# Retention in chunks of 64 tokens: four products on quarters of the PE array, a compact state summed by DVE

## The chip, the cores and the metric

One Trainium2 chip, one of its cores. A time is the device time of one execution in microseconds (us); smaller is better. The kernel before takes 1517.68 us, the median of three runs (1516.84 to 1517.86). TensorE is called PE in the profile, VectorE DVE, ScalarE ACT, GpSimd POOL, and SyncE, which issues the DMAs, SP.

## What is computed

Eight batches of eight heads, 576 tokens, head size 64. Retention is attention without softmax, with a decay that depends on the head; two mixing layers follow.

```python
scores = scale * np.matmul(q, k.transpose(0, 1, 3, 2))
Dmat = np.where(rel >= 0, gamma[:, None, None] ** rel[None, :, :], 0.0)   # rel = pos_i - pos_j
x = np.matmul(scores * Dmat, v)                    # heads side by side: B, S, 512
u = x + (x.transpose(0, 2, 1) @ U @ V).transpose(0, 2, 1)        # U: 576x32
x = u + np.maximum(u @ w_ch1, 0.0) @ w_ch2                       # 512 -> 2048 -> 512
xk, xr = (mu * x + (1 - mu) * x_prev for mu in (mu_k, mu_r))     # x_prev: the token before
out = sigmoid(xr @ w_r) * ((np.maximum(xk @ w_k, 0.0) ** 2) @ w_v)
```

## The kernel before

Tokens are numbered through all batches (T = 4608) and cut into nine blocks of 512 for the dense layers. Every dense product is made of three fp32r products (high x high, low x high, high x low), so weights and activations are split into a high and a low part first. The weights arrive as 64-bit numbers. `convert` (lines 88 to 125) turns one 128x512 piece into the two parts in four stages: `load` (DMA), `flush` (one ACT instruction), `fill` (four DVE instructions, L103 to L113) and `split` (ACT, then a subtraction on POOL). `slot()` starts the next waiting piece and moves each running piece one stage on. All engines take their instructions in the order in which the program is written (a manual schedule).

The retention stage (lines 294 to 651) runs over chunks of 128 tokens, four full ones and a tail of 64 per batch. First comes a sequence in which batches 0 and 1 alternate, chunk by chunk, then batches 2 to 7 one after the other. For one chunk:
- `load_chunk` brings q and k transposed (two heads, 64 rows each, on the partitions) and k and v with tokens on the partitions; `scale_v` (L338, POOL) multiplies v by gamma to the power of minus the position.
- `scores` (L350): eight products of 64x128 by 64x128, the two heads of a pair on the two row halves of the array, each head pair into its own place in two banks; DVE multiplies the two banks by a causal mask into `pm` (L359).
- `inter` (L398): four products with the state of a head pair, a 128x128 tile `wst` that is zero off its two diagonal blocks; `intra` (L414): eight products of v and `pm` added onto the same bank. DVE multiplies the sum with `qtab` (the positive powers) into `xt` (L424).
- `state` (L376): eight products of k and v, accumulated in PSUM over the whole batch, copied by ACT into the diagonal blocks of `wst` after each chunk (L385).
- `natural` (L432): four transposes of `xt`, copied by ACT (L442); `low_rank` (L452): four products with U, each into its own 32 partitions.

fp32 matmuls appear as two records each (16 for eight products); a transpose and an fp32r matmul appear as one.

After a batch's last chunk `low_rank_sum` and eight `mix` steps (L479: a product with V on PE, an addition on DVE, L483) give u, and `mix_store` splits u (`split_u`, L188 on ACT and L189 on DVE) and stores it. From then on the block's 16 `hidden` tiles are ready: each is 12 matmuls of 128x512 (L201), a relu on ACT and a store. In the order of the program (`chunk_step`) 18 hidden tiles are put between the steps of a batch's five chunks: 4, 4, 4, 3 and 3, behind `inter`; with the second chunk the eight mixes go between the parts of hidden tiles. In the first 11 steps (`first`) there are no hidden tiles, and each step ends with one or two `slot()`. After batch 7 five more hidden tiles go with its last transposes, low rank and mixes. The rest of the hidden tiles and the later layers (lines 653 to 780) are not touched by the change, except that they get their PSUM from a second pool.

The eight PSUM banks are: 0 and 1 hidden tiles, 2 and 3 scores, 4 the retention output, 5 the state, 6 transposes and mixes, 7 low rank.

## Time and profile before

| | us |
|---|---|
| median of three runs | 1517.68 (1516.84 to 1517.86) |
| the profiled execution | 1516.35 |
| its span, first to last instruction | 1514.6 |
| PE busy, share of the span | 1475.2 (97%) |
| DVE busy | 590.3 (39%) |
| ACT busy | 517.2 (34%) |
| POOL busy | 242.2 (16%) |
| mean granted TensorE clock | 0.983 |

How to read the rows further down: busy time is the union of the records of an engine, and PE's records overlap where matmuls are pipelined, so the cost of a group on PE is the distance from its first start to the first start of what follows. In a row of the timeline the first number is the start, the second the time to the end of the last record, and xN the number of records merged into the row; what stands in square brackets is idle time of the engine before it and what ended it.

### The profile page before, as it was taken

Reading aid. Unit: us, or ns where it says so; the run is one execution under the profiler, and the core shown is the slowest. Engines: PE = TensorE matmul, PEld = TensorE weight load, DVE = VectorE, ACT = ScalarE, POOL = GpSimd, SP = SyncE. Lnnn points to the kernel's source line nnn. Section 1 sums busy time; section 2 is a strip of 40 time slices with the busy share of each in tenths; the row PEclk is TensorE's granted clock in tenths of the full one; section 3 lists DMA queues with packets and bytes.
Section 4 is the critical chain, followed back from the end, with each engine's and each line's share of the span. In section 5 each row is a group of like instructions: output and inputs, shape, how many; then the busy total and the mean of one; then the engine's idle time right before and its main releaser. Section 6 shows DMA issues by size and latency. Waiting matters only on the chain. (4 is left out here: it accounts for less than half of the span.)

```text
span 1514.6 us, 20307 instructions
## 1 busy us (share of the span) xinstructions
PE 1475.2 (97%) x8220; PEld 1210.2 (80%) x8220; DVE 590.3 (39%) x868; ACT 517.2 (34%) x903; POOL 242.2 (16%) x216
## 2 busy tenths in 40 slices
PE   7889999999999999999999999998999999999999
PEld 5667888888888778888888888786888888888887
DVE  5965312131212166585222322285442442343241
ACT  2443323232223344433111211244443444444441
POOL 3422101001010032131000000014202201211220
PEclk8879999999999999999999999999999999999999
DMA  9634544344443356775334554343110110110000
GB/s 331 231 121 144 182 134 160 133 163 139 148 153 140 128 174 209 249 236 179 124 121 149 167 160 158 126 139 98 56 55 8 49 56 14 42 56 22 8 28 28
DMA packets 77822, 190.03 MB, mean 125 GB/s; under 512 B 10592, under 2 KB 19040, under 8 KB 77728
## 3 DMA queue, kind: packets, MB, share of 16 engines
q1 hardware_dynamic: 77728, 188.73, 37.1%
q8 instruction: 64, 1.05, 0.3%
q14 instruction: 30, 0.25, 0.1%
HBM read 122.64 MB, written 66.06 MB: 125 GB/s over the span
## 5 line engine op out<-in xcount | busy, mean ns | idle before, releaser
L207 ACT ACTIVATE hs<-h 128x512 f32<-128x512 f32 x144 | 85.8, 597 | 263.4 <-PE h L201 256.4
L221 ACT CAST hh<-hr 128x1024 fp32r<-128x1024 f32 x72 | 75.7, 1051 | 232.6 <-DVE hl L222 65.1
L730 POOL TENSOR_TENSOR kl<-ks,kh 128x512 fp32r<-128x512 f32 x72 | 93.8, 1304 | 354.9 <-ACT kh L729 353.2
L222 DVE TENSOR_TENSOR hl<-hr,hh 128x1024 fp32r<-128x1024 f32 x72 | 87.6, 1223 | 159.7 <-PE c L235 101.4
L424 DVE TENSOR_TENSOR xt<-x,qtab 128x512 f32<-128x512 f32 (+1 forms) x40 | 25.4, 636 | 238.1 <-PE x L414 237.4
L760 DVE TENSOR_TENSOR o<-v,g 128x512 f32<-128x512 f32 x36 | 24.9, 692 | 185.8 <-PE v L756 185.8
L728 DVE SCALAR_TENSOR_TENSOR ks<-k,ka 128x512 f32<-128x512 f32 x72 | 49.7, 690 | 117.5 <-ACT ka L726 68.5
L338 POOL TENSOR_TENSOR kv<-kv,vtab 128x512 f32<-128x512 f32 (+1 forms) x40 | 45.6, 1143 | 277.9 <-DMA kv<-in_qkv 217.2
L288 ACT CAST mh<-m 128x512 fp32r<-128x512 f32 x72 | 44.8, 623 | 115.4 <-DVE tp L281 82.6
L729 ACT CAST kh<-ks 128x512 fp32r<-128x512 f32 x72 | 44.5, 621 | 56.7 <-DVE ks L728 56.7
L108 DVE SCALAR_TENSOR_TENSOR cf<-cf,ca 128x512 uint32<-128x512 uint32 (+3 forms) x56 | 60.7, 1085 | 1.9
L284 DVE SCALAR_TENSOR_TENSOR m<-x2l,mu,tp 128x512 f32<-128x512 f32 x72 | 53.7, 750 | 13.5 <-ACT tp L275 6.2
L359 DVE TENSOR_TENSOR pm<-s,mask 128x512 f32<-128x512 f32 (+1 forms) x80 | 47.1, 630 | 28.2 <-PE s L350 28.2
L350 PE MATMUL s<-qk 64*128 64x128 f32 (+1 forms) x640 | 47.4, 285 | 10.9 <-DVE pm L359 5.7
L252 POOL COPY edge<-x 128x1 f32<-128x1 f32 x36 | 14.5, 403 | 270.6 <-DVE x L251 270.6
L275 ACT ACTIVATE tp<-x2l,omu 128x511 f32<-128x511 f32 x72 | 51.5, 715 | 17.8 <-DMA x2l<-xb 17.8
L234 PE MATMUL c<-hh,w_1h 128*128 128x512 f32 x144 | 56.3, 391 | 0.6 <-ACT hh L221 0.6
L726 ACT ACTIVATE ka<-k 128x512 f32<-128x512 f32 x72 | 42.8, 597 | 40.5 <-PE k L722 39.5
L235 PE MATMUL c<-hh,w_1l 128*128 128x512 f32 x144 | 56.1, 389 | 0.0
L234 PE MATMUL c<-hh,w_0h 128*128 128x512 f32 x144 | 56.0, 389 | 0.0
L235 PE MATMUL c<-hh,w_0l 128*128 128x512 f32 x144 | 56.0, 389 | 0.0
L234 PE MATMUL c<-hh,w_2h 128*128 128x512 f32 x144 | 56.0, 389 | 0.0
(152 smaller groups left out, 3408.5 us busy)
## 6 DMA issues: line engine op xcount, KB each, us to landing
hb<-hs SPq DMA_DIRECT2D x144, 256.0 KB, 2.0
hr<-hb SPq DMA_DIRECT2D x72, 512.0 KB, 4.9
qk<-in_qkv SPq DMA_DIRECT2D x32, 512.0 KB, 5.2
kv<-in_qkv SPq DMA_DIRECT2D x32, 512.0 KB, 5.8
w_raw<-in_moe_w_ch SPq DMA_DIRECT2D x32, 512.0 KB, 4.7
ur<-ub SPq DMA_DIRECT2D x18, 512.0 KB, 4.5
xb<-x SPq DMA_DIRECT2D x36, 256.0 KB, 3.3
x2l<-xb SPq DMA_DIRECT2D x18, 512.0 KB, 4.5
```

What stands on the lines that cost most here:

```text
L108: nc.vector.scalar_tensor_tensor(f.bitcast(U32), f.bitcast(U32), 0xC0000000, a.bitcast(U32), op0=ALU.bitwise_and, op1=ALU.bitwise_or,)
L207: nc.scalar.activation(h, hps.pop((t, f)), AF.Relu)
L221: nc.scalar.copy(h, r)
L222: nc.vector.tensor_tensor(l, r, h.bitcast(F32), op=ALU.subtract)
L234: nc.tensor.matmul(acc[t][o], w.part(0, f % 4, oo), hh, start=(f == 0), stop=False)
L235: nc.tensor.matmul(acc[t][o], w.part(1, f % 4, oo), hh, start=False, stop=False)
L275: nc.scalar.activation(tp[:, 1:], xk[:, :BT - 1], AF.Copy, scale=omu[:, j, k:k + 1])
L284: nc.vector.scalar_tensor_tensor(m, xk, mu[:, j, k:k + 1], tp, op0=ALU.mult, op1=ALU.add)
L350: nc.tensor.matmul(ps[g][:n, a, :n], t[r, 1, a * n:(a + 1) * n], t[r, 0, a * n:(a + 1) * n], start=True, stop=True, skip_group_check=True,)
L359: nc.vector.tensor_tensor(p[:n, g, :, :n], ps[g][:n, :, :n], mask[:n, :, :n].to_broadcast([n, NP, n]), op=ALU.mult,)
L728: nc.vector.scalar_tensor_tensor(sq, ps, 0.0, a, op0=ALU.max, op1=ALU.mult)
L730: nc.gpsimd.tensor_tensor(kl, sq, kh.bitcast(F32), op=ALU.subtract)
```

## The change

Chunks have 64 tokens, nine per batch. q, k and v are laid out anew on the host side of the launch, so that the halves of the partitions hold the two heads of a pair for q and k (swapped for every second pair), and two groups of heads for k and v with tokens. All four products are of 64x64 by 64 columns, eight per chunk, and consecutive ones go to the four quarters of the array in turn. Scores and inter of a chunk share a pair of banks (`up`), state and intra another (`dn`), each single. k instead of v is scaled by POOL. DVE multiplies the scores with a table that holds mask, decay and scale (`decay`), and in `leave` makes y (inter times `qtab`), the new state (the old one plus this chunk's product, in SBUF, 128 x 4 x 64 without zeros) and the output (intra plus y). ACT no longer copies the state. Of `qtab` only the first fifth is loaded, POOL multiplies it up.

The sequence starts with four chunks of batch 0, then batches 1 and 0 alternate, so that batch 0 ends at step 13 of 18; batch 1 ends at 17. Each step has two hidden tiles, one behind the products and one behind the transposes or the low rank product, which go over the pairs of chunks (128 tokens) and are put off by one and by two to four steps. Mixes go between the parts of whatever hidden tiles come next.

```diff
+L = 64
+NL = S // L
...
-    big = ctx.enter_context(tc.tile_pool(name="big", bufs=32))
+    big = ctx.enter_context(tc.tile_pool(name="big", bufs=34))
-    psum = ctx.enter_context(tc.tile_pool(name="psum", bufs=1, space=PSUM))
...
+    first_psum = ctx.enter_context(ExitStack())
+    psum.append(first_psum.enter_context(tc.tile_pool(name="psa", bufs=1, space=PSUM)))
...
+        dtab = ac.tile([128, 2, 2, L], F32, name="dtab")
+        step = ac.tile([128, NP, 1], F32, name="step")
+        ktab = ac.tile([128, NC, 2, NP, 1], F32, name="ktab")
+        qk, kv = {}, {}
+        def load(b, p):
+            n = 2 if p < NC - 1 else 1
+            qk[b, p] = unit(big, F32, f"qk{b}_{p}")
+            nc.sync.dma_start(qk[b, p][:, :n], io["qk"][b, :, 2 * p:2 * p + n])
+            kv[b, p] = unit(big, F32, f"kv{b}_{p}")
+            nc.sync.dma_start(kv[b, p][:, :n], io["kv"][b, :, 2 * p:2 * p + n])
+        def scale_k(b, p):
+            n = 2 if p < NC - 1 else 1
+            k = kv[b, p][:, :n, :256].rearrange("p c (h d) -> p c h d", d=D)
+            nc.gpsimd.tensor_tensor(k, k, ktab[:, p, :n].to_broadcast([128, n, NP, D]), op=ALU.mult)
+        def qkt(b, c, x, r, a):
+            o = x * 256 + a * L
+            return qk[b, c // 2][r, c % 2, o:o + L]
+        def kvn(b, c, x, r, a, g):
+            o = x * 256 + (a // 2) * 128 + g * D
+            return kv[b, c // 2][r, c % 2, o:o + D]
+        half = (slice(0, 64), slice(64, 128))
+        up, down = {}, {}
+        wst = {}
+        xt = {}
+        def pair(nm, i):
+            return psum[0].tile([128, 2, 512], F32, tag=nm, name=f"{nm}{i}", bufs=1)
+        def scores(i):
+            b, c = seq[i]
+            t = up[i - 1] = pair("up", i)
             for a in range(NP):
                 for g in range(2):
+                    r = half[(g + a) % 2]
                     nc.tensor.matmul(
+                        t[half[a % 2], g, (a // 2) * L:(a // 2 + 1) * L],
+                        qkt(b, c, 1, r, a),
+                        qkt(b, c, 0, r, a),
+                        start=(a < 2),
...
+        def decay(i):
+            t = up[i - 1] if i else up.pop(-1)
+            m = pm[i] = a2.tile([128, 2, 2, L], F32, tag="pm", name=f"pm{i}")
+            nc.vector.tensor_tensor(
+                m, t[:, :, 0:128].rearrange("p g (a i) -> p g a i", i=L), dtab, op=ALU.mult
+            )
+        def inter(i):
+            b, c = seq[i]
+            if c > 0:
+                new = i not in up
+                if new:
+                    up[i] = pair("up", i)
+                for a in range(NP):
+                    for g in range(2):
+                        r = half[(g + a) % 2]
+                        nc.tensor.matmul(
+                            up[i][half[g], a % 2, 128 + (a // 2) * L:128 + (a // 2 + 1) * L],
+                            wst[b][r, a],
+                            qkt(b, c, 0, r, a),
...
+        def own(i):
+            b, c = seq[i]
+            t = down[i] = pair("dn", i)
+            if c < NL - 1:
+                for a in range(NP):
+                    for g in range(2):
+                        r = half[a % 2]
+                        nc.tensor.matmul(
+                            t[half[(g + a) % 2], a % 2, 128 + (a // 2) * D:128 + (a // 2 + 1) * D],
+                            kvn(b, c, 0, r, a, g),
+                            kvn(b, c, 1, r, a, g),
...
+            p = pm.pop(i)
+            for a in range(NP):
+                for g in range(2):
+                    r = half[a % 2]
+                    nc.tensor.matmul(
+                        t[half[g], a % 2, (a // 2) * L:(a // 2 + 1) * L],
+                        kvn(b, c, 1, r, a, g),
+                        p[r, g, a // 2],
...
+        def by_pair(x):
+            return x.rearrange("p (a r) i -> p a r i", r=2)
+        def leave(i):
+            b, c = seq[i]
+            u, t = up.pop(i, None), down.pop(i)
+            if c == 0:
+                xt[b] = a2.tile([128, KD, S], F32, tag="xt", name=f"xt{b}", bufs=3)
+            o = (c % 2) * L
+            x = by_pair(xt[b][:, :, c * L:(c + 1) * L])
+            if c > 0:
+                y = a2.tile([128, NP, L], F32, tag="y", name=f"y{i}", bufs=1)
                 nc.vector.tensor_tensor(
+                    by_pair(y),
+                    u[:, :, 128:256].rearrange("p r (a i) -> p a r i", i=L),
+                    by_pair(qtab[:, c // 2, :, o:o + L]),
                     op=ALU.mult,
                 )
+            if c < NL - 1:
+                d = t[:, :, 128:256].rearrange("p r (a x) -> p a r x", x=D)
+                new = a2.tile([128, NP, D], F32, tag="wst", name=f"w{b}_{c}", bufs=4)
+                if c == 0:
+                    nc.vector.tensor_copy(by_pair(new), d)
+                else:
+                    nc.vector.tensor_tensor(by_pair(new), d, by_pair(wst[b]), op=ALU.add)
+                wst[b] = new
+            own_x = t[:, :, 0:128].rearrange("p r (a i) -> p a r i", i=L)
             if c == 0:
+                nc.vector.tensor_copy(x, own_x)
+            else:
+                nc.vector.tensor_tensor(x, own_x, by_pair(y), op=ALU.add)
...
+        def natural(b, p):
...
+        gall = []
+        def low_rank(b, p):
+            n = CH[p][1]
+            if not gall:
+                gall.append(bank("g", "gall"))
...
                 nc.tensor.matmul(
+                    gall[0][32 * k:32 * k + 32, 128 * (b % 4):128 * (b % 4) + 128],
...
+                    start=(p == 0 and b % 4 == 0),
+                    stop=(p == NC - 1),
...
+            ps = turn("m", ("n", 0, 1), f"mx{b}_{k}_{s}") if b == 0 else bank("n", f"mx{b}_{k}_{s}")
+        def hidden(n):
...
+                    m = bool(todo)
                     for part in range(3):
                         hidden_part(t, f, part)
+                        mixes(1)
                     if not m:
                         slot()
...
+        LEAD = 4
+        seq = [(0, c) for c in range(LEAD)]
+        for c in range(NL - LEAD):
+            seq += [(1, c), (0, c + LEAD)]
+        seq += [(1, c) for c in range(NL - LEAD, NL)]
+        seq += [(b, c) for b in range(2, B) for c in range(NL)]
+        N = len(seq)
+        FIRST = 2 * NL
+        units = []
+        for i, (b, c) in enumerate(seq):
+            if c % 2 == 0:
+                units.append((i, b, c // 2))
...
+        def load_to(i):
+            while units and units[0][0] <= i:
+                load(*units.pop(0)[1:])
+        load_to(0)
+        nc.sync.dma_start(dtab, io["dtab"])
+        nc.sync.dma_start(ktab, io["ktab"])
+        nc.sync.dma_start(qtab[:, 0], io["qtab"])
+        nc.sync.dma_start(step, io["step"])
+        load_to(2)
+        scale_k(0, 0)
+        scores(0)
+        decay(0)
+        load_to(5)
+        for p in range(1, NC):
+            nc.gpsimd.tensor_tensor(
+                qtab[:, p], qtab[:, p - 1], step.to_broadcast([128, NP, C]), op=ALU.mult
+            )
+        due = {}
+        def plan(i, fn, *args):
+            due.setdefault(i, []).append((fn, args))
+        def step_of(i):
+            first = i < FIRST
+            load_to(i + (7 if first else 4))
+            if i + 1 < N:
+                nb, ncx = seq[i + 1]
+                if ncx % 2 == 0:
+                    scale_k(nb, ncx // 2)
+            if i + 1 < N:
+                scores(i + 1)
+            inter(i)
+            if i + 1 < N:
+                decay(i + 1)
+            own(i)
+            leave(i)
+            if c % 2 == 1 or c == NL - 1:
+                wait = 4 if i < 8 else 2
+                plan(i + 1, natural, b, c // 2)
+                plan(i + wait, low_rank, b, c // 2)
+                if c == NL - 1:
+                    plan(i + wait, low_rank_sum, b)
+                    plan(i + wait + 1, later, b)
+            if first and (i < 10 or i % 2 == 0):
+                slot()
+            if not ready:
+                mixes(4)
+            hidden(1)
+            for fn, args in due.pop(i, []):
+                fn(*args)
+            hidden(1)
+        for i in range(N):
+            step_of(i)
+        for i in sorted(due):
+            for fn, args in due.pop(i):
+                fn(*args)
+            hidden(2)
+        while todo:
+            hidden(1) if ready else mixes(1)
...
+    first_psum.close()
+    psum.append(ctx.enter_context(tc.tile_pool(name="psb", bufs=1, space=PSUM, reuse_waits="tile")))
```

## Rows read from the trace of the kernel before

**Rows 1.** Windows: busy us (records) of PE, PEld, DVE, ACT, POOL; clock; DMA share; GB/s.
```profile
0.00:25.00 25.00, 16.61 (x180) 11.70 (x180) 10.71 (x23) 5.21 (x11) 6.29 (x12) 0.93 0.94 341
25.00:50.00 25.00, 20.80 (x234) 17.12 (x236) 20.30 (x31) 11.35 (x26) 10.16 (x8) 0.80 1.00 325
50.00:75.00 25.00, 21.15 (x256) 17.46 (x252) 24.22 (x33) 11.84 (x24) 11.02 (x8) 0.82 0.47 186
75.00:100.00 25.00, 18.82 (x100) 14.74 (x101) 17.83 (x28) 9.04 (x18) 7.57 (x6) 0.64 0.30 97
...
200.00:250.00 50.00, 50.00 (x357) 40.67 (x355) 10.22 (x19) 15.20 (x30) 5.46 (x5) 1.00 0.41 135
```

**Rows 2.** Timeline of PE: the first hidden tile.
```profile
90.92 2.05 PE L201 MATMUL h<-uh,w_0h 128*128 128x512 f32 x4
```

**Rows 3.** PE's waits up to 130 us: total, times, longest.
```profile
PE s L350 <- DVE pm L359: 5.7, 4, 2.1
PE xn L432 <- DVE xt L424: 5.0, 2, 3.5
...
PE xn L432 <- DVE xt L483: 4.1, 1, 4.1
```

**Rows 4.** Timeline of PE: from batch 5's first chunk, and batch 6's first product.
```profile
303.59 0.69 PE L376 MATMUL ds<-kv 128*64 128x64 f32 x16
304.11 1.05 PE L414 MATMUL x<-pm,kv 128*64 128x128 f32 x16
305.08 0.42 PE L452 MATMUL g<-xs,ust 64*32 64x128 f32 x8
305.43 1.16 PE L350 MATMUL s<-qk 64*128 64x128 f32 x16
306.53 0.66 PE L432 MATMUL xn<-ident,xt 128*128 128x128 f32 x4
307.02 1.06 PE L398 MATMUL x<-qk,wst 128*128 128x128 f32 x8
307.83 1.18 PE L201 MATMUL h<-uh,w_1h 128*128 128x512 f32 x4
...
373.82 0.69 PE L376 MATMUL ds<-kv 128*64 128x64 f32 x16
```

**Rows 5.** Timeline of PE: a run of four hidden tiles.
```profile
108.56 1.18 PE L201 MATMUL h<-uh,w_0h 128*128 128x512 f32 x4
...
110.49 1.07 PE L201 MATMUL h<-ul,w_0h 128*128 128x512 f32 x4
...
113.21 1.07 PE L201 MATMUL h<-ul,w_0h 128*128 128x512 f32 x4
...
119.65 0.69 PE L376 MATMUL ds<-kv 128*64 128x64 f32 x16
```

**Rows 6.** Timeline of PE: the 64-token tail's intra and what follows.
```profile
149.57 0.68 PE L414 MATMUL x<-pm,kv 64*64 64x64 f32 x16
150.18 0.43 PE L452 MATMUL g<-xs,ust 128*32 128x128 f32 x8
```

**Rows 7.** Timeline of PE around the start of one low rank product.
```profile
305.08 0.31 PE L452 MATMUL g<-xs,ust 64*32 64x128 f32 x4
```

**Rows 8.** Groups by form: count, busy us, mean ns, idle before.
```profile
L452 PE MATMUL g<-xs,ust 128*32 128x128 f32 x256 | 14.1, 293 | 4.0 <-ACT xs L442 4.0
```

**Rows 9.** Timeline of DVE: conversions, masks and output between 50 and 60 us.
```profile
53.17 1.28 DVE L359 TENSOR_TENSOR pm<-s,mask 128x512 f32<-128x512 f32 x2
54.37 0.68 DVE L424 TENSOR_TENSOR xt<-x,qtab 128x512 f32<-128x512 f32 x1
54.97 1.70 DVE L103 SCALAR_TENSOR_TENSOR cf<-ca,w_raw 128x512 f32<-128x512 f32 x1
...
59.22 0.74 DVE L359 TENSOR_TENSOR pm<-s,mask 64x256 f32<-64x256 f32 x2
```

**Rows 10.** Timeline of ACT: the split of batch 0's u.
```profile
83.92 2.61 ACT L188 CAST uh<-xt 128x1024 fp32r<-128x1024 f32 x4 [0.79 <-DVE xt L483]
```

More of the change, by code (lines that the diff above doesn't have):

```diff
@@ L340, in retention_mixer_kernel @@
-        pm = {}
-        def scores(b, c):
-            n = CH[c][1]
-            t = qk.pop((b, c))
-            p = a2.tile([128, 2, NP, C], F32, tag="pm", name=f"pm{b}_{c}")
-            ps = [bank(2 + g, f"s{b}_{c}_{g}").rearrange("p (a i) -> p a i", a=NP) for g in range(2)]
+        qk, kv = {}, {}
[5 more added lines that the diff above has]
+            nc.sync.dma_start(kv[b, p][:, :n], io["kv"][b, :, 2 * p:2 * p + n])
@@ L357, in scores @@
                     )
-            for g in range(2):
+        def decay(i):
[17 more added lines that the diff above has]
+                            qkt(b, c, 0, r, a),
+                            start=(new and a < 2),
+                            stop=True,
+                            skip_group_check=True,
+                        )
@@ L389, in retention_mixer_kernel @@
-        xt = {}
-        xb = {}
-        def inter(b, c, q):
-            n = CH[c][1]
-            x = xb[b, c] = bank(4, f"x{b}_{c}").rearrange("p (a i) -> p a i", a=NP)
-            if c > 0:
-                for a in range(NP):
-                    nc.tensor.matmul(
-                        x[:, a, :n],
-                        wst[2 * (b % 2) + c % 2][:, a, :],
-                        q[:, 0, a * n:(a + 1) * n],
-                        start=(a == 0),
-                        stop=False,
-                        skip_group_check=True,
-                    )
@@ L510, in later @@
             todo.append(lambda: mix_store(b))
-        def hidden(n, m=0):
+        def hidden(n):
             for _ in range(n):
@@ L642, in retention_mixer_kernel @@
-        for i in range(LAST + 1):
-            chunk_step(i)
-        natural(*seq[-1])
-        hidden(1)
-        low_rank(*seq[-1])
-        low_rank_sum(B - 1)
-        later(B - 1)
-        hidden(1)
-        hidden(3, 1)
-        mixes(1000)
+        scale_k(0, 0)
[5 more added lines that the diff above has]
+                qtab[:, p], qtab[:, p - 1], step.to_broadcast([128, NP, C]), op=ALU.mult
+            )
```

227 lines of the change are left out of this document (45 added, 182 removed).

## Prediction

> **What bounds the kernel now.** I read three views in this order: the windows (how busy each engine is by stretch), TensorE's waits, and its timeline. The windows [rows 1] show two regimes. Up to about 90 us PE is busy for 17 to 21 us of each 25, with a granted clock of 0.93 down to 0.64, while DVE is busy 20.3 and 24.2 us of the second and third 25. From there on PE is full: 50.00 of 50 us at clock 1.00, DVE 10.2. So a microsecond of TensorE time counts one for one after 90 us, and before it what counts is when the first hidden matmul can start (90.92 us) [rows 2]. Until then PE waits longest for the masked scores, for the scaled retention output and for the mix sums [rows 3]. DVE makes all three, and in its program the conversion of the 64-bit weights stands between these steps.
>
> **Steady part, before.** From the state product of batch 5's first chunk at 303.59 to that of batch 6 at 373.82 [rows 4] one batch takes 70.23 us. In it are 18 hidden tiles. One hidden tile of 12 matmuls takes 2.72 (110.49 to 113.21) [rows 5], 48.96 for all, so 21.27 us go to everything else. By rows 4 a full chunk has state 0.52 (start to next start), intra 0.97, low rank 0.35, scores 1.10, transposes 0.49 and inter 0.81. The tail of 64 tokens has 64x64 products: intra takes 0.61 [rows 6]. Entering and leaving a run of hidden tiles costs 0.21: 48 matmuls from 108.56 to 119.65 are 11.09, against 4 x 2.72 = 10.88 [rows 5].
>
> **Steady part, after.** What goes: the four retention products of a batch, 4 x (0.52 + 0.97 + 1.10 + 0.81) + 1.2 for the tail's two 64x64 products = 14.8 us and more. What comes: 9 chunks of four products, less the inter of the first and the state of the last, 34 products of 8 quarters, each quarter two records (the trace counts 16 for 8 fp32 matmuls): 16 records each. Their price is not in the trace, since no row has all four quarters in use; the nearest rows bound it. State now sends 16 records of 64 columns through two column halves in 0.52, that is 0.065 for a concurrent pair. If four quarters run together for what two halves take, a product has four rounds, 4 x 0.065 = 0.26; if only two run together it has eight, 0.52. The low rank product decides which end I take: it puts four tiles side by side, its first four matmuls all lie within one stretch of 0.31 us [rows 7], and its 8 records of 128 columns take 0.35 with the mode change behind them, against 0.81 for the 8 full-array records of inter. So four tiles cost about what one does, and I take 0.26. What stays unknown is that the quarters split rows and columns at once, which low rank doesn't.
>
> 34 x 0.26 = 8.8 us. Each chunk now breaks the hidden run for its products (0.21) and changes the array's shape at its end (0.09, the tail's intra 0.61 against 0.52 for as many columns): 9 x 0.30 = 2.7. Transposes and low rank move out into a second break per chunk: 5 x (0.49 + 0.06) and 5 x (0.35 + 0.21) = 5.6. Mixes and small change stay, 1.4. The sum is 18.5 against 21.3: 2.7 us less per batch, 16 us over batches 2 to 7. With 0.065 down to 0.058 a round it is 19; with two at a time it is 8.8 us more, 18.5 + 8.8 = 27.3, or 36 us slower over six batches.
>
> The records must also be started fast enough; the densest stretch of the trace is state's, 16 in 0.52 or 0.032 each, and 0.26 wants one each 0.016. Low rank speaks for it: one of its matmuls takes 0.293 [rows 8] and four together 0.31 [rows 7], so that different tiles start about 0.006 apart; I add nothing. The Trainium skill, "TensorEngine Tiling (Array Packing)", Instruction Overhead, speaks against the change: about 60 cycles for each matmul, so that one should not take a tiling factor from a dimension that is already small. An estimate by that page, 60 cycles at 2.4 GHz = 25 ns, one after the other for 34 x 16 records, would be 13.6 us instead of 8.8 and leave 2 us of loss per batch in place of the gain. The starts of low rank's four don't agree with such a floor between tiles; a longer dense stretch is not in the trace.
>
> **The start.** On DVE, masks and output scaling (per full chunk 1.28 for the two masked scores and 0.68 for the output) [rows 9] give way to four instructions of 256 columns per 64 tokens: decay, y, state sum, output. Their price is the row of two 64x256, 0.74, that is 0.37 each. By the first hidden tile 19 chunks need 19 x 4 x 0.37 = 28 us; before, 9 pairs of masks, two tails and ten outputs (eight of 0.68, two of half the size) took 11.5 + 1.5 + 6.2 = 19. DVE gets 9 us more. Against that: DVE has 14.3 idle us in the first 25 [rows 1]; the state no longer passes through ACT, which in its order also takes raw weights; low rank is put off by up to four steps, so that its copy holds PE less; and the tables lose 1.05 MB of 1.3, 3 us at 341 GB/s. POOL's four new table products (about 1.0 us each, as its scaling) lie in that idle time too. I take 7 of the 9 as absorbed: +2. Ends: nothing absorbed, +9; all absorbed and the 3 us of loads besides, -3. In addition the first hidden tile stands at chunk 19 of 64 tokens instead of after 10 full steps plus one of 128, so one chunk of 64, about 2 us, is still to do: +2. Weights: as many conversions as before lie ahead of it, so they cancel.
>
> **The end of the retention.** With two hidden tiles in every chunk from chunk 19, 106 are used by chunk 71 and 6 of block 6 remain; the flush uses two each for transposes, low rank and the mixes, and the last two mixes, the store and the split of batch 7 stand with nothing in front of them. Today 109 are used then and the 3 left cover the split. Two mixes of about 0.8 us (an estimate: matmul, wait and an add of 0.4), one more add and two casts (four take 2.61) [rows 10] are 3.6 us, and I take 5 with a colder clock behind the gap (rows 1 show 0.64 where PE had gaps). Ends 3 and 8. Elsewhere PE waits for nothing new: the single up and down pairs are read within 2 us and a chunk has two hidden tiles, 5.4 us, between reuse. Loads keep their size; the DMA is at 41% [rows 1].
>
> **The sum.** The profiled execution took 1516.35 (span 1514.6), 1.33 below the median of 1517.68. 1516.35 - 16 + 2 + 2 + 5 = 1509.35; with 1.33 for the median 1510.7, say 1510.5.
>
> **Rivals.** (a) Quarters go two at a time. For: no row shows rows and columns split at once; and if records can't be started faster for long than in state (0.032), the price is the same, 16 x 0.032 = 0.52. Against: low rank's four [rows 7]. Time: 1517.7 + 36 + 9 = 1563; a partial overlap (0.39 a product, 4.4 us more per batch) gives 1537. (b) DVE becomes the bound, the case on the slower side. From chunk 19 the seven weight conversions still missing come at two per chunk, 4.25 us each as from 54.97 to 59.22 [rows 9]: 4 x 0.37 + 2 x 4.25 = 10 us against 7.3 of PE per chunk. It decides from where DVE's queue is more than a chunk behind, since the decay of the next scores then lies behind a conversion: four chunks x 2.7 = 11, less the 3.5 that PE waits today in that place [rows 3], with all 9 us of the start: -16 + 9 + 2 + 7.5 + 5 gives 1525. The Trainium skill names it: "TensorEngine Tiling (Array Packing)", PSUM Bottleneck, says that after a faster TensorE the copies out of PSUM may become the bound. No row shows that after 200 us (DVE 10.2 of 50); before 90 us DVE already is. (c) The ends cost nothing: -19 - 3 + 2 + 3 gives 1500.
>
> **How the numbers follow.** Forecast 0.5, with a third of it within the mark below; (a) 0.12; (b) 0.18; (c) 0.2. Likeliest: 1510.5. The range leaves out (a) beyond its partial form and the far side of (c): 1497 to 1534. About 0.2%, 3 us, is what a measurement can tell here. Faster: two thirds of the forecast and (c), 0.53; same: the last third, 0.17; slower: (a) and (b), 0.30.
>
> **What would show it.** Right: in the timeline after, each product's 16 records within about 0.26 us and the four of a chunk in 1.1; a batch in about 67.5 instead of 70.2; first hidden tile at 91 to 95; a gap of 3 to 6 us where batch 7 is split. Wrong: products of 0.5 (a); PE waiting for decay or the state sum after 95 us (b); a first hidden tile before 88 (c).

## The result and the profile after

The changed kernel takes 1496.67 us (median of four runs, 1495.31 to 1497.27) against 1517.26 for the kernel before in the same comparison: ratio 0.9864, 95% interval 0.9847 to 0.9881. That is 20.6 us less; 1510.5 was forecast and the range ended at 1497. The profiled execution has a span of 1493.4 us, 21.2 less than before.

The windows of the kernel after, by the columns of [rows 1] (busy us and records of PE, PEld, DVE, ACT, POOL; granted clock; DMA share; GB/s):

```profile
0.00:25.00 25.00, 15.21 (x324) 10.21 (x324) 10.48 (x29) 3.05 (x6) 8.45 (x12) 0.79 0.94 347
25.00:50.00 25.00, 14.72 (x399) 12.23 (x399) 24.20 (x48) 9.32 (x18) 7.77 (x6) 0.57 0.97 349
50.00:75.00 25.00, 16.75 (x492) 12.86 (x492) 22.75 (x45) 9.30 (x18) 12.37 (x11) 0.82 0.33 129
75.00:100.00 25.00, 18.81 (x250) 13.69 (x251) 21.36 (x37) 11.20 (x22) 6.56 (x6) 0.86 0.39 125
...
200.00:250.00 50.00, 50.00 (x632) 38.76 (x630) 11.71 (x30) 12.78 (x25) 4.40 (x4) 1.00 0.38 133
```

There are still two regimes. From 25 to 50 us DVE is now full (24.20 of 25, 20.30 before), PE is idle for 10 us and its granted clock is 0.57 (0.80 before), close to the lower of the two levels, 1.2 GHz. After 200 us PE is full at clock 1.00 as before; DVE has 11.71 of 50 us where it had 10.22.

The timeline of PE after, for what [rows 2] and [rows 4] showed: the first hidden tile, the beginnings of batches 5 and 6, and one chunk between them (start, us, what, count):

```profile
86.30 0.73 PE L204 MATMUL h<-uh,w_0h 128*128 128x512 f32 x2 [0.52 <-ACT uh L191]
...
285.31 0.46 PE L358 MATMUL up<-qk 64*64 64x64 f32 x16
...
300.13 0.46 PE L358 MATMUL up<-qk 64*64 64x64 f32 x16
300.41 0.41 PE L383 MATMUL up<-qk,w 64*64 64x64 f32 x16
300.64 0.41 PE L399 MATMUL dn<-kv 64*64 64x64 f32 x16
300.88 0.41 PE L411 MATMUL dn<-pm,kv 64*64 64x64 f32 x16
301.22 1.19 PE L204 MATMUL h<-uh,w_2h 128*128 128x512 f32 x4
...
352.31 0.46 PE L358 MATMUL up<-qk 64*64 64x64 f32 x16
```

The first hidden tile stands at 86.30 instead of 90.92. A batch takes 352.31 - 285.31 = 67.00 us instead of 70.23. The four products of a chunk take 1.09 (300.13 to 301.22): from start to start 0.28 for the first, 0.23 for the next two, and 0.34 for the last with the way back to the hidden tile.

**Where the 21 us lie.** The scores of batch 3's first chunk start at 144.28 (150.54 before), those of batch 7's at 412.29 (431.54), each time with 14 and 86 hidden tiles done in both kernels; the first product of the projection starts at 596.96 (617.98). So 6.3 us are gained up to batch 3, 13.0 over the four batches to batch 7 (3.25 each), 1.8 from there to the projection. If batches 2 and 7 gain 3.25 too, the steady part gives 19.5, the start 3.0, and the end of the retention costs 1.5. Behind 596.96 both kernels need the same (896.4 and 896.6). The start of the projection is used below to compare traces: all of the retention and all hidden tiles lie ahead of it.

The end of the retention after, on ACT and PE (the last mixes of batch 7, then the first tile of block 7):

```profile
505.30 1.43 ACT L191 CAST uh<-xt 128x128 fp32r<-128x128 f32 x3
...
505.50 0.41 PE L508 MATMUL mx<-vst,gt 96*128 96x320 f32 x1 [0.58 <-DVE xt L512]
...
506.49 0.41 PE L508 MATMUL mx<-vst,gt 96*128 96x320 f32 x1 [0.58 <-DVE xt L512]
...
506.74 1.09 PE L204 MATMUL h<-uh,w_0h 128*128 128x512 f32 x4
```

PE waits twice, 0.58 us each, and goes on with hidden work right behind the last mix: the casts for block 7 (64 tokens from the first segment) began at 505.30, while the last mixes of the second segment were still running.

DVE in the start, four retention instructions of one chunk between two conversion steps:

```profile
29.89 0.42 DVE L370 TENSOR_TENSOR pm<-up,dtab 128x256 f32<-128x256 f32 x1
30.23 0.41 DVE L432 TENSOR_TENSOR y<-up,qtab 128x256 f32<-128x256 f32 x1
30.56 0.41 DVE L444 TENSOR_TENSOR w<-dn,w 128x256 f32<-128x256 f32 x1
30.89 0.41 DVE L450 TENSOR_TENSOR xt<-dn,y 128x256 f32<-128x256 f32 x1
31.22 1.31 DVE L106 SCALAR_TENSOR_TENSOR cf<-ca,w_raw 128x512 f32<-128x512 f32 x1
```

Each is shown as 0.42, but they overlap at their ends: 0.333 from start to start, against the 0.37 that the forecast took.

### The profile page after: what moved, and what is told of

The parts are those of the page before. It is cut to its first block, busy times and chain, and to the rows that moved or that the text cites. A ratio compares the mean times of both kernels' runs of the same rounds, so it can differ in the third digit from the quotient of the medians.

```text
span 1493.4 us, 25018 instructions
## 1 busy us (share of the span) xinstructions
PE 1443.6 (97%) x10524; PEld 1164.9 (78%) x10524; DVE 611.7 (41%) x1020; ACT 491.2 (33%) x839; POOL 239.0 (16%) x216
## 5 line engine op out<-in xcount | busy, mean ns | idle before, releaser
L370 DVE TENSOR_TENSOR pm<-up,dtab 128x256 f32<-128x256 f32 x72 | 30.4, 423 | 206.6 <-PE up L383 171.5
L329 POOL TENSOR_TENSOR kv<-kv,ktab 128x512 f32<-128x512 f32 (+1 forms) x40 | 41.0, 1028 | 199.6 <-DMA kv<-in_kv 164.3
L358 PEld LDWEIGHTS up<-qk 64*64 64x64 f32 x1152 | 26.3, 145 | 41.8 <-issue 32.5
L111 DVE SCALAR_TENSOR_TENSOR cf<-cf,ca 128x512 uint32<-128x512 uint32 (+3 forms) x56 | 56.8, 1014 | 1.9
L512 DVE TENSOR_TENSOR xt<-mx,xt 128x256 f32<-128x256 f32 (+1 forms) x64 | 28.8, 457 | 68.8 <-PE mx L508 68.7
L794 PE MATMUL v<-wv_0h,kl 128*128 128x512 f32 x144 | 56.1, 390 | 0.0
L238 PE MATMUL c<-hh,w_3l 128*128 128x512 f32 x144 | 56.1, 390 | 0.0
```

Of the source, the lines that this page charges most:

```text
L111: nc.vector.scalar_tensor_tensor(f.bitcast(U32), f.bitcast(U32), 0xC0000000, a.bitcast(U32), op0=ALU.bitwise_and, op1=ALU.bitwise_or,)
L238: nc.tensor.matmul(acc[t][o], w.part(1, f % 4, oo), hh, start=False, stop=False)
L794: nc.tensor.matmul(ps, x[:, f % 2, io_], wv[f // 4].part(lo, f % 4), start=(j == 0), stop=(j == len(ops) - 1))
```

## The experiments

All are edits to the changed kernel. "Projection" is the start of its first product, "batch" the distance between two batches' first scores, "first tile" the first hidden matmul, all from the profiled execution, that is from one execution each. The changed kernel's was the fastest of its four (1495.31), and the first tiles of e3_slot16 and e11_best, whose programs differ ahead of it by one low rank product alone, lie 1.0 us apart. So differences of about 1 us in first tile and projection tell nothing; the batch is steadier (66.94 to 67.05 in the nine runs that leave it alone).

| run | median us | ratio to before, 95% | first tile | batch | projection |
|---|---|---|---|---|---|
| before | 1517.26 | | 90.92 | 70.23 | 617.98 |
| changed kernel | 1496.67 | 0.9864 (0.9847 to 0.9881) | 86.30 | 67.00 | 596.96 |
| e1_two | 1506.44 | 0.9934 (0.9919 to 0.9949) | 86.21 | 68.46 | 606.57 |
| e5_diag | 1545.43, one run | | 90.58 | 75.29 | 646.31 |
| e2_grouped | 1498.67 | 0.9877 (0.9861 to 0.9894) | 86.15 | 65.30 | 599.91 |
| e3_slot16 | 1494.45 | 0.9850 (0.9835 to 0.9865) | 82.34 | 66.94 | 594.90 |
| e4_extra | 1501.83 | 0.9901 (0.9886 to 0.9916) | 89.14 | 67.00 | 599.84 |
| e6_tables | 1498.66 | 0.9894 (0.9877 to 0.9910) | 89.11 | 66.96 | 600.32 |
| e7_alternate | 1497.92 | 0.9885 (0.9871 to 0.9900) | 95.93 | 66.96 | 600.08 |
| e8_noscale | 1495.96 | 0.9872 (0.9857 to 0.9887) | 85.97 | 66.96 | 596.68 |
| e9_wait2 | 1499.38 | 0.9890 (0.9875 to 0.9905) | 87.06 | 67.05 | 599.49 |
| e10_undone | 1502.01 | 0.9910 (0.9894 to 0.9926) | 96.67 | 67.00 | 602.10 |
| e14_both | 1502.90 | 0.9910 (0.9894 to 0.9927) | 92.33 | 67.00 | 603.97 |
| e11_best | 1481.79 | 0.9778 (0.9761 to 0.9795) | 81.37 | 65.30 | 584.35 |
| e12_few | 1485.54 | 0.9799 (0.9785 to 0.9814) | 82.13 | 65.27 | 585.75 |
| e13_ahead | 1481.22 | 0.9767 (0.9753 to 0.9782) | 79.24 | 65.29 | 582.48 |

### Do four quarters run together?

e1_two, in all four products:

```diff
-            for a in range(NP):
-                for g in range(2):
+            for g in range(2):
+                for a in range(NP):
```

> In the changed kernel the eight quarter products of a step are issued so that any four in a row use all four quarters of the array. Here the two loops around them are swapped in all four products: the same instructions, but any four in a row use two quarters only (for scores and the state the two on a diagonal, for inter and intra two row halves of one column half). Theory (four quarters run at once, and this is what brings the steady gain): a product takes about 0.46 us instead of 0.23, so 34 x 0.23 = 7.8 us more per batch, 74.8 instead of 67.0 from batch to batch, and about 8 x 7.8 = 62 us less what hides in the start: some 1545 us, slower than the kernel before. Rival (quarters go two at a time anyway, or what limits is how fast records are sent, and the gain is from the smaller chunk alone): a product stays at 0.23, the batch at 67.0, the time at 1497.

Timeline of PE in e1_two, one chunk:

```profile
298.13 0.47 PE L358 MATMUL up<-qk 64*64 64x64 f32 x16
298.42 0.42 PE L383 MATMUL up<-qk,w 64*64 64x64 f32 x14
298.65 0.22 PE L399 MATMUL dn<-kv 64*64 64x64 f32 x1
298.67 0.22 PE L383 MATMUL up<-qk,w 64*64 64x64 f32 x2
298.71 0.36 PE L399 MATMUL dn<-kv 64*64 64x64 f32 x10
298.88 0.22 PE L411 MATMUL dn<-pm,kv 64*64 64x64 f32 x1
298.90 0.22 PE L399 MATMUL dn<-kv 64*64 64x64 f32 x3
...
299.41 0.96 PE L204 MATMUL h<-uh,w_1h 128*128 128x512 f32 x3
```

Neither held. The four products take 1.28 (298.13 to 299.41) instead of 1.09, a batch 1.46 more, not 7.8. The rows show why the edit was too weak: the first state record (L399) starts at 298.65, ahead of the last two inter records (L383, 298.67) that were issued before it, and intra and state mix in the same way. By the program that state record goes to another quarter than the two inter records. So in these rows a record whose quarter is free starts ahead of older ones whose quarters are not, and the order of issue decides little.

e5_diag therefore takes two of the quarters away (scores shown; in inter, state and intra the row half is likewise made to follow the column half):

```diff
-                    r = half[(g + a) % 2]
+                    r = half[a % 2]
```

> All four products use only the two quarters on the array's diagonal: each quarter product reads the row half that equals the column half it writes to. Instructions, columns and order stay; half of the products read the wrong half of the data, so that part of the computation is changed. Theory (each quarter runs one record per 0.058 us by itself, and four at once are what makes a product take 0.23): two quarters need eight rounds, 8 x 0.058 = 0.47 per product, 34 x 0.24 = 8 us more per batch (75 instead of 67.0) and some 1550 us in all, given that the two-quarter order of the run before cost 1.46 per batch and 10 in all. Rival (the number of records that are sent sets the time, whichever quarter they go to): a product stays at 0.23 to 0.29, the batch at 67 to 68.5.

Timeline of PE in e5_diag, one chunk:

```profile
318.07 0.73 PE L358 MATMUL up<-qk 64*64 64x64 f32 x16
318.58 0.68 PE L383 MATMUL up<-qk,w 64*64 64x64 f32 x16
319.05 0.68 PE L399 MATMUL dn<-kv 64*64 64x64 f32 x16
319.51 0.68 PE L411 MATMUL dn<-pm,kv 64*64 64x64 f32 x16
320.13 0.50 PE L204 MATMUL h<-uh,w_1h 128*128 128x512 f32 x1
```

The same 16 records now take 0.47 (318.58 to 319.05), twice 0.23, the batch 75.29 (8.29 more) and the one run 1545. The theory named 0.47, 75 and some 1550. It is shown: with four quarters a product has four rounds of 0.058 us, with two it has eight, and the number of records alone doesn't set the time. Without the four quarters the change would be slower than the kernel before.

### What a break costs

e2_grouped:

```diff
-            if not ready:
-                mixes(4)
-            hidden(1)
             for fn, args in due.pop(i, []):
                 fn(*args)
-            hidden(1)
+            if not ready:
+                mixes(4)
+            hidden(2)
```

> Transposes and low rank products run straight behind the chunk's products and not between its two hidden tiles, so that the hidden run is broken once per chunk. Theory (a break costs 0.2 us by itself, as the forecast has it): 5 to 6 breaks less in each batch, 0.2 each, so the batch goes from 67.0 to 65.8 and the time from 1496.7 to about 1489. Rival (what costs is the change of shape between the 64x64 products, the 128 wide transposes and the 32 wide low rank, and that change stays): batch 66.6 to 67.0, time within 2 us of 1496.7. Second rival: the transposes now stand behind the retention output that DVE has only just begun (about 0.7 us of sums), and PE waits for it: 5 x 0.5 us more per batch, 1510.

The steady part gave what a break of 0.2 makes and more, 65.30 a batch (1.70 less, some 0.3 for each of the five or six breaks). But the time didn't fall: up to batch 3 it is 5.0 us behind the changed kernel (batch 3's first scores at 154.75, with two tiles more done), where PE waits 3.2 us for ACT's casts of u instead of 1.2, where 19 chunks and not 20 lie ahead of its first tile, so that one more is still to do, and where PE's granted clock from 100 to 125 us is 0.83 instead of 0.93 (its row stands further down). How much each of these makes isn't settled. And at the end its hidden tiles are used up too early. Timeline of PE in e2_grouped at the end of the retention, eight mixes with nothing between them:

```profile
501.23 0.28 PE L508 MATMUL mx<-vst,gt 96*128 96x256 f32 x1
502.03 0.38 PE L508 MATMUL mx<-vst,gt 96*128 96x256 f32 x1 [0.52 <-DVE xt L512]
...
508.16 0.64 PE L508 MATMUL mx<-vst,gt 96*128 96x320 f32 x1 [0.58 <-DVE xt L512]
508.60 1.91 PE L204 MATMUL h<-uh,w_0h 128*128 128x512 f32 x4
```

From 501.23 to 508.60 the mixes and PE's waits for DVE's adds (seven of 0.5 to 0.6 us) have 7.4 us to themselves, 0.92 a mix; the changed kernel has two such waits. The forecast's gap of 3 to 8 us was another one, two mixes, the store and the split: even here hidden work starts 0.44 behind the last mix (508.16), so that PE doesn't wait for the split.

### What bounds the start

e3_slot16 moves one conversion step behind the first tile; e4_extra, in the second diff, gives DVE 19 instructions more:

```diff
-            if first and (i < 10 or i % 2 == 0):
+            if first and (i < 10 or i in (10, 12, 14)):
                 slot()
```

> One weight conversion step of the start (four DVE instructions, 2.8 to 4.7 us) is moved behind the first hidden tile: no conversion slot at chunk 16. Theory (before 86 us DVE's program order is the bound): the first hidden tile comes 2.8 to 4.7 us sooner than 86.30, at 81.6 to 83.5; in the time 2 to 4 us appear, if the conversion then hides beside hidden tiles: 1493 to 1495. Rival (the start is bound by PE at a low granted clock, or by when the raw weights come from DRAM): the first hidden tile stays at 86 and the time within 1 us.

```diff
+            if i <= FIRST:
+                nc.vector.tensor_tensor(
+                    m, t[:, :, 0:128].rearrange("p g (a i) -> p g a i", i=L), dtab, op=ALU.mult
+                )
```

> The decay instruction is issued twice in the first 19 chunks (same operands, same result): 19 DVE instructions of 128x256 more, 0.333 us from start to start each. Theory (DVE is the bound of the start): first hidden tile 19 x 0.333 = 6.3 us later, at 92.6, and the time 1503. Rival (my forecast's absorption: most of added DVE work lies in idle time; DVE is idle for 21 of the first 86 us): 1 to 2 us later, time 1498. If the first holds, the forecast's 7 of 9 us absorbed was wrong and the gain of the start came from work that went away; if the rival holds, it was the price of the added work that was wrong.

e3_slot16 brings the first tile 4.0 us forward and the projection 2.1. e4_extra pushes the projection back by 2.9, 0.46 of the 6.3 us that were added: between theory and rival. (Its profiled execution, 1499.50, was the fastest of four; the median is 5.2 above the changed kernel's, nearer to the theory.) DVE in e4_extra up to 25.7 us, when the first raw weights are in (groups by line and shape; busy, mean ns, idle before):

```profile
L374 DVE TENSOR_TENSOR pm<-up,dtab 128x256 f32<-128x256 f32 x6 | 2.5, 424 | 0.2
L370 DVE TENSOR_TENSOR pm<-up,dtab 128x256 f32<-128x256 f32 x6 | 2.5, 422 | 8.1 <-DMA dtab<-in_dtab 5.6 <-PE up L387 1.9 <-PE up L358 0.7
```

Six of the 19 lie there, where DVE waits for tables and for PE anyway (8.3 us in these two rows); the other 13 are 4.3 us, and 2.9 came through.

e8_noscale takes POOL's work away beside DVE:

```diff
-                if ncx % 2 == 0:
+                if ncx % 2 == 0 and nb > 1:
                     scale_k(nb, ncx // 2)
```

(the first call, for batch 0, is left out too.)

> POOL's scaling of the keys is left out for batches 0 and 1 (12 instructions, 13.5 us of POOL; their state and so their output are wrong). In the trace a DVE conversion step of 128x512 takes 0.69 us with POOL idle beside it and up to 1.7 us with POOL at work. Theory (POOL slows DVE in the start, and where they happen to meet decides some us): conversions fall from 36.2 us to about 31, the first hidden tile comes 2 to 4 us sooner than 86.30, time 1493 to 1495. Rival (the slow steps have other causes, or lie beside the path): first hidden tile within 1 us of 86.30 and the time too.

The rival held for the time. Groups of DVE up to 86 us, first two of the changed kernel, then the same two of e8_noscale:

```profile
L370 DVE TENSOR_TENSOR pm<-up,dtab 128x256 f32<-128x256 f32 x21 | 8.8, 420 | 12.6 <-DMA dtab<-in_dtab 5.5 <-PE up L383 4.7 <-PE up L358 2.5
...
L107 DVE TENSOR_SCALAR ca<-cf 128x512 uint32<-128x512 uint32 x9 | 7.0, 774 | 0.3
```

```profile
L370 DVE TENSOR_TENSOR pm<-up,dtab 128x256 f32<-128x256 f32 x21 | 8.8, 420 | 15.3 <-PE up L383 7.4 <-DMA dtab<-in_dtab 5.4 <-PE up L358 2.5
...
L107 DVE TENSOR_SCALAR ca<-cf 128x512 uint32<-128x512 uint32 x9 | 5.5, 613 | 0.3
```

The conversions do get faster (L107 from 774 to 613 ns), but what DVE saves it waits for PE's scores and inter: idle before the decay rises from 12.6 to 15.3. In this stretch PE and DVE hand the chunk to each other, and less work on DVE alone gained nothing here. It isn't so in every place: the step that e3_slot16 moves stood just ahead of the first tile, and there 4.0 us were gained.

### Undoing the parts of the start

e6_tables loads the table whole, e7_alternate takes back the lead, e9_wait2 the delay of the low rank products:

```diff
+            if b == 0 and p > 0:
+                nc.sync.dma_start(qtab[:, p], io["qtab"])
...
-        for p in range(1, NC):
-            nc.gpsimd.tensor_tensor(
-                qtab[:, p], qtab[:, p - 1], step.to_broadcast([128, NP, C]), op=ALU.mult
-            )
```

> One part of the change is undone: the table that scales the outputs is loaded whole from DRAM, 256 KB ahead of each of batch 0's loads, in place of POOL's four products from the first part (the loads bring the first part each time, so that the later chunks are scaled by the wrong values). Theory (the start gained by less to load: the chain to the first hidden tile leaves the transfers at 31.5 us before and at 25.7 after): 1.05 MB at 331 GB/s is 3.2 us, so the first hidden tile comes 3 us later than 86.30 and the time is 1499 to 1500. Rival (the loads are not the bound, DVE's order is, and POOL's four products of 1.04 us only disturb DVE): first hidden tile at 86 or up to 2 us sooner, time 1495 to 1497.

```diff
-        LEAD = 4
+        LEAD = 1
```

> One part of the change is undone: the chunks of batches 0 and 1 alternate from the beginning, as in the kernel before, so that batch 0 has no lead of four chunks. Batch 0 is then complete three chunks later, and its mixes stand three chunks later. Theory (the lead brings the first hidden tile forward and with it the gain of the start): first hidden tile 2 to 6 us later than 86.30, time 1499 to 1502. Rival (both batches have to be done anyway and the same work only changes places): first hidden tile up to 4 us later but the time within 1 us of 1496.7.

```diff
-                wait = 4 if i < 8 else 2
+                wait = 2
```

> One part of the change is undone: in the first eight chunks a low rank product follows two steps behind its chunk, as later, and not four. Theory (the delay keeps PE from waiting for ACT's copy of the transposes, behind which raw weights stand in ACT's order): PE waits for the copy 3 to 4 times for about 0.5 us each, first hidden tile 1 to 2 us later than 86.30, time 1498. Rival (PE waits there for DVE and for the loads anyway): first hidden tile within 0.5 us and time within 1 us of the changed kernel's 0.9864 of before.

The projection comes 3.4 us later with the tables loaded, 3.1 without the lead, 2.5 without the delay. In the medians it is 2.0, 1.3 and 2.7. (Without the lead the first tile is even 9.6 us later, but more retention is done by then, 23 chunks and not 20: batch 3 begins after 8 hidden tiles, not 14.) For the tables the rows show the way. ACT's first two steps on raw weights, waiting for the DMA, in the changed kernel and then in e6_tables:

```profile
21.88 0.66 ACT L100 ACTIVATE ca<-w_raw 128x512 f32<-128x512 f32 x1 [13.78 <-DMA w_raw<-in_moe_w_ch]
25.71 0.67 ACT L100 ACTIVATE ca<-w_raw 128x512 f32<-128x512 f32 x1 [2.70 <-DMA w_raw<-in_moe_w_ch]
```

```profile
22.94 0.66 ACT L100 ACTIVATE ca<-w_raw 128x512 f32<-128x512 f32 x1 [14.76 <-DMA w_raw<-in_moe_w_ch]
27.84 0.67 ACT L100 ACTIVATE ca<-w_raw 128x512 f32<-128x512 f32 x1 [3.76 <-DMA w_raw<-in_moe_w_ch]
```

The second raw weight comes 2.1 us later and all conversions behind keep that. For the delay of the low rank products the size is measured, but not the way. The theory's waits aren't it: before 25 us PE waits once for ACT's copy in either kernel, 4.6 us in e9_wait2 and 3.3 in the changed kernel, but batch 2's first scores come no later for it (71.10 and 71.44). The loss lies behind, 0.8 us at the first tile and 1.8 more up to batch 3. From 71 to 150 us PE's waits are alike (10.1 and 10.6 us in all), and its granted clock isn't. Windows of the changed kernel, e9_wait2 and e2_grouped, by the columns of [rows 1]:

```profile
100.00:125.00 25.00, 22.39 (x275) 17.18 (x276) 16.83 (x31) 7.70 (x14) 3.19 (x3) 0.93 0.47 162
100.00:125.00 25.00, 21.33 (x212) 16.16 (x216) 15.67 (x27) 7.35 (x14) 3.61 (x3) 0.86 0.39 126
100.00:125.00 25.00, 19.66 (x197) 14.41 (x196) 16.39 (x28) 6.70 (x12) 4.02 (x3) 0.83 0.39 137
```

A clock lower by 0.07 over 25 us is about 1.8 us, an estimate and as much as e9_wait2 loses there. What lowered it wasn't tried.

e10_undone has these three diffs together.

> All three parts of the start are undone together: the output table loaded whole, batches 0 and 1 alternating from the first chunk, low rank two steps behind. The runs with one part undone gave +3.4 us of first tiles' time for the table and +3.1 for the order. Theory (they are separate costs and add up, and with them the start's gain of 5.9 us is explained): the hidden tiles from the 24th on lie 6 to 7.5 us later than in the changed kernel, the time is 1502.5 to 1504. Rival (loads and DVE bound the same stretch, whichever ends last, so the parts overlap): 3.5 to 4.5 us later, 1500, and some 2 us of the gain still come from something else in the start.

Together 5.1 us instead of 9.0 at the projection, between theory and rival in the trace, while the median came near the theory (1502.0). In the trace, then, the parts overlap; the medians don't show it (6.0 for the three alone, 5.3 together), so that this isn't settled. Either way they are more than the 3.0 us that the start gained: what is left of the change in the start costs about 2.

e14_both has the diffs of e6_tables and e4_extra in one kernel.

> Two edits of earlier runs together in the changed kernel: the output table loaded whole (1.05 MB more; the later chunks scaled by wrong values), which alone moved the tiles of the steady part by 3.3 us, and the decay issued twice in the first 19 chunks (6.3 us of DVE), which alone moved them by 2.9. Theory (in the start loads end last and DVE work is free as far as it waits for them): the two overlap, 3.5 to 4.5 us in all. Rival (once the first raw weights are there DVE has no gap left, so that a later raw weight and more DVE work both count): they add up, 5.5 to 6.5 us.

They add up: 7.0 us at the projection against 3.4 + 2.9, and in the medians 6.2 against 2.0 + 5.2. Neither hides the other here. The reading that fits: the loads fix when the first raw weights are there, and from then on DVE's order counts.

### A faster version

e11_best joins the grouped run from batch 2 on, the moved conversion step of e3_slot16, and a flush of one, two and three tiles:

```diff
-            hidden(1)
+            hidden(1 if first else 0)
             for fn, args in due.pop(i, []):
                 fn(*args)
-            hidden(1)
+            hidden(1 if first else 2)
...
-        for i in sorted(due):
+        for n, i in enumerate(sorted(due)):
             for fn, args in due.pop(i):
                 fn(*args)
-            hidden(2)
+            hidden(n + 1)
```

> Three edits to the changed kernel together: from batch 2 on the transposes and low rank products run directly behind the chunk's products (the grouped run: 1.45 us less per batch from tile 24 to 96, but 3 us lost in the start and 3.6 more at the end, which this version avoids by leaving the start as it is); no conversion slot at chunk 16 (2.2 us); and in the last steps of the retention one hidden tile beside the transposes, two beside low rank and three beside the mixes, so that all eight mixes have hidden work between them (two waits of 0.58 us today). Theory: 6 x 1.45 + 2.2 + 1.2 = 12 us below the changed kernel, some 1484.5, ratio to before about 0.978. Rival (the parts don't add up: the split of the last batch waits for the adds that are now later, 2 to 4 us): 1487 to 1489.

The parts added up: 12.6 us at the projection, 1481.79 us, ratio 0.9778. It beats both kernels. e12_few has no slot at chunk 14 either (the edit against e11_best):

```diff
-            if first and (i < 10 or i in (10, 12, 14)):
+            if first and (i < 10 or i in (10, 12)):
                 slot()
```

> The version of the three edits, with one more conversion slot of the start moved behind the first hidden tile (none at chunk 14). Theory (each slot moved brings the first tile 4 us forward, as the first did, and 2.2 us in the time, while PE has hidden tiles to run): 2 us below the three edits, 1482.5. Rival (the second group of weights is needed by the ninth tile; four conversions of 2.8 to 4.3 us of DVE then stand beside eight tiles of 2.72 us, and PE waits for the weights): no gain, or up to 3 us loss.

Not a gain but a loss (1.4 us at the projection, 3.7 in the median), on the rival's side, though not by its reason, since the first tile itself comes no sooner (82.13). DVE's waits for inter from 25 to 82 us (total, times, longest), in e11_best and then in e12_few:

```profile
DVE pm L370 <- PE up L383: 2.6, 5, 1.0
```

```profile
DVE pm L370 <- PE up L383: 5.7, 6, 2.2
```

With one conversion less ahead of the first tile DVE only waits longer for PE, as in e8_noscale. What makes PE late there wasn't tried; its largest wait in that stretch, ahead of the scores (7.3 us in e11_best, 6.5 in e12_few), is one for which the profile shows no releaser.

e13_ahead changes the order of the loads in e11_best:

```diff
-            load_to(i + (7 if first else 4))
+            load_to(i + (5 if first else 4))
```

> The version of the three edits with one more: in the start the batches' loads are issued five chunks ahead and not seven, so that each raw weight stands behind one load pair (1 MB) less in the queue. In the changed kernel ACT waits for the first raw weight until 21.88 us and for the second until 25.71, and all conversions behind keep that offset. Theory (the loads end last in the start): raw weights land up to 3 us sooner, the first hidden tile 2 to 3 us sooner than the 81.37 of the three edits, time 1479 to 1480. Rival (DVE's order ends last, or the chunks now wait for their own loads): first hidden tile within 1 us or later, time 1481 to 1484.

ACT in e13_ahead:

```profile
18.83 0.67 ACT L100 ACTIVATE ca<-w_raw 128x512 f32<-128x512 f32 x1 [10.69 <-DMA w_raw<-in_moe_w_ch]
```

The first raw weight is worked on 3.7 us sooner than in e11_best (22.52), the first tile comes 2.1 sooner and the projection 1.9, as the theory has it. In the time it can't be told from e11_best: the intervals 0.9753 to 0.9782 and 0.9761 to 0.9795 overlap.

## Why the prediction was right and wrong

The direction and the main mechanism were right, the size was not: 13.8 us of gain were missing, and they fall on three terms.

**Steady part: right, mis-sized by 3.5 us.** Forecast 16 us over six batches, measured 19.5 (3.25 a batch). A product has four rounds and takes 0.23, not 0.26: a round is 0.058, the value that the forecast named as the other end. That is 34 x 0.03 = 1.0 a batch; 3.25 of the 3.7 that this makes came, and where the rest went isn't settled. The forecast's own 19 for that end is a slip: 34 x 4 x 0.007 = 0.95 a batch is 5.7 over six batches, which makes 22 and not 19. The step from low rank to quarters, "four tiles cost about what one does", held for rows and columns split at once, as e5_diag shows. The price put on rival (a) was of the right size too: 1563 with 0.52 a product, and e5_diag has 1545 with 0.47. The Trainium skill, "TensorEngine Tiling (Array Packing)", Instruction Overhead, has about 60 cycles for each matmul, an estimate of 25 ns at 2.4 GHz. As a floor from one start to the next, which is how the forecast's estimate took it for each record, the trace doesn't bear it out on different quarters: 16 records, of eight matmuls, start within 0.23 us, 14 ns each. On one quarter a record takes 0.058 us, which is above it.

**Start: wrong in sign, 7 us.** Forecast +4, measured -3.0 (if batch 2 gains 3.25 as the others do). Two steps failed. First "I take 7 of the 9 as absorbed": the 3 us of loads that the tables lose were put among what absorbs, though by [rows 1] the DMA engines were at 0.94 and 1.00 of their time up to 50 us. The forecast read PE and DVE in that view and not the DMA share beside them. And among PE's waits before, from which [rows 3] are taken, one for the loads stands ahead of the mix sums that the forecast names:

```profile
PE s L350 <- DMA qk<-in_qkv: 4.9, 2, 3.0
```

With a full queue 1.05 MB less are 3 us at their full price, and e6_tables measured 3.4. The low rank delay (2.5) stood in the same sum without a price.

Second "one chunk of 64 is still to do, about 2 us: +2", which is a miscount. Intra ahead of the first hidden tile, of the kernel before and then of the kernel after (16 records a chunk):

```profile
L414 PE MATMUL x<-pm,kv 128*64 128x128 f32 x144 | 11.6, 311 | 0.0
L414 PE MATMUL x<-pm,kv 64*64 64x64 f32 x32 | 1.8, 271 | 0.0
```

```profile
L411 PE MATMUL dn<-pm,kv 64*64 64x64 f32 x320 | 12.3, 270 | 2.0 <-issue 2.0
```

Nine chunks of 128 and two tails are 1280 tokens, and so are 20 chunks of 64 (step 19, counted from 0, is the twentieth): nothing more is left to do, and DVE's 28 us are a chunk short for the same reason. The lead of batch 0 is in the forecast only through this count; e7_alternate, with 23 chunks ahead of the first tile, shows what it is worth, 3.1 at the projection (1.3 in the median).

The three parts together are 5.1 (e10_undone). What remains, about +2, has the size that the forecast gave to DVE's added work, but that it is this work isn't shown. Added DVE work does cost (e4_extra: 0.46 of it in the trace), at 0.333 and not 0.37 for each instruction. The forecast's own mark spoke early: "a first hidden tile before 88 (c)", and it came at 86.30.

**End of the retention: mechanism wrong, 3.5 us.** Forecast +5, measured +1.5. The step that failed is "stand with nothing in front of them": the last mixes do run bare, twice 0.58, but the hidden tiles of block 7 need only the first segment of batch 7, whose adds are long done, and ACT casts it before the last mixes end. The price of a mix, 0.8, was near (0.92 in e2_grouped); a wait for the store and the split came in neither run, and the colder clock only behind the longer gap of e2_grouped (granted 0.77 from 500 to 515 us, 1.00 in the changed kernel).

**The rivals.** (c), the ends cost nothing, 1500, was nearest. With the two slips put right (22 for 19, no chunk left to do) it would have been 1517.7 - 22 - 3 + 3 = 1496 and the end of the range below it; that this is the measured time is partly luck, since the terms measured 19.5, 3.0 and 1.5. (b), DVE as the bound after 95 us, didn't come: from 95 to 490 us PE waits neither for decay nor for the state sum, only for mixes and one cast (2.1, 1.4 and 0.4 us), and from 200 on it is busy 50.00 of 50 us and DVE 11.71.

## What to carry to other kernels

Where a start has several bounds, read the DMA share of the same windows as the engines: with the queues full, 1.05 MB of loads were worth about their transfer time here, and more DVE work came on top of it. Before work is booked as still to do, count the tokens that are done by then in both kernels. Ask of each item at an end what exactly the next tile needs, one segment or the whole. Small products pay on quarters of the array if each product has work for all four; with two quarters the gain of 21 us here became a loss of 30 (1545.43 against 1515.85 in the same comparison, one run). And each break of a long run has its price: five to six breaks less in a batch gave 1.70 us.

## What was not expected of the hardware

Records of small products pass each other: in e1_two a state record starts at 298.65 ahead of inter records issued before it (298.67), so swapping the order of issue cost only 0.19 us per four products.

A DVE conversion step of 128x512 depends on what POOL does beside it: L107 has a mean of 774 ns in the start and 613 with POOL's scalings gone. It moved neither the first tile nor the time.

In the start the change lowered PE's granted clock: 0.57 from 25 to 50 us against 0.80 [rows 1], with PE busy 14.72 of 25 us instead of 20.80. From 75 to 100 us it is the other way round, 0.86 against 0.64. The start got shorter all the same.
